# A third bank for the sums of the row maxima, three output banks in place of four, and one more query buffer, in the front of a two-branch attention kernel

## The chip, the cores and the metric

The kernel runs on one core of one Trainium2 chip. The metric is the device time of one execution in microseconds (us). Before the change the median of three runs is 1454.08 us (1453.64 to 1454.22). The profile is of another execution, which took 1453.78 us; its span, from the first to the last instruction, is 1452.0 us. About 0.2%, or 2.9 us, is what a measurement of this kernel can tell from no change.

## The reference

There are 2048 positions and a model width of 512, with 32 heads of 16. Branch A is attention over 8 dilated neighbours of each position; branch B has 32 query heads and one shared key and value head over all 2048 positions. A sigmoid gate mixes the two.

```python
qkv = (x @ wqkv).reshape(B, S, 3, H, Dh).transpose(2, 0, 3, 1, 4)
idx = pos[:, None] - (arange(8) * 2)[None, :]          # branch A: 8 positions, 2 apart
logits = where(idx >= 0, einsum("bhsd,bhswd->bhsw", q, k[idx]) * scale, -1e9)
a = (softmax(logits) @ v[idx]) @ wo

scores = einsum("bhqd,bkd->bhqk", x @ wq, x @ wk) * Dh ** -0.5   # branch B
b = (softmax(scores) @ (x @ wv)) @ wo_b
return g * a + (1 - g) * b                             # g = sigmoid(x . gate_w)
```

## The kernel before

**The units of branch B.** The 2048 queries times 32 heads are 32 units; a unit's queries stand in one buffer `qst[place(u)]`, 128 partitions by 2 x 512. Its upper and its lower 64 partitions hold different queries, so TensorE works on them as two independent row halves: a matmul of one half runs beside a matmul of the other. Before the exponentials of a unit can run, the maximum of its scores over all keys must be known; it is subtracted inside the matmul by two more rows of `qst`. So each unit needs 64 *half scores*: a 128 x 512 block of scores (four blocks of keys, four of queries, two banks of heads, two halves), and the maximum of each row of it. There are 2048 of these.

**Three ways to fill a half score.** A *pair* (`fill_pair`, bank `pm`) is two half scores, one for each row half, and one VectorE reduction of 128 x 1024 (line 365). A *single* (`fill_one`, mostly bank `ps`, that is `m1`) is one matmul on one half and one reduction of 128 x 512 (line 377). A *difference and sum* handles two half scores of the same row half together: a matmul against `kd`, the difference of two blocks of keys (`fill_diff`, line 414, banks `pd`), a Relu of it by ScalarE into a held buffer `dd` (line 426), then a matmul of the second block (`fill_sum`, line 343, banks `ps` or `po`) and one custom VectorE instruction that adds the two and takes the maximum (line 438, followed by a short read of the accumulator). Two matmuls and two half scores in every case; only the difference and sum needs one VectorE instruction for two half scores of one row half.

**The front.** The projections come first: the queries of branch B (13 lumps after the first three) and q, k, v of branch A (64 lumps), each lump 12 products of a split in three terms, each product one matmul for either row half. `front_stream` writes out TensorE's order by hand: it keeps a model clock for each row half and at each point either takes the next projection matmul of that half (`mm`, line 1136) or a fill (`pick`), if by its model a bank is free, the buffers are there and VectorE and ScalarE are not behind. The projections accumulate in four output banks in turn, `fb[x % 4]` (`home`); the upper half of lump x waits until lump x - 4 has left its bank (`below`). Sums of the upper row half use `m1`, those of the lower half `po`. Differences use two banks of their own, `pd`. The numbers at the top of the file (`T_EXP`, `T_TTR` and so on) are the planner's durations; they put no instruction into the program, but they decide its order. Units that have been queued with `stack` can be filled; nine buffers `qst` and one more, `qstx`, stand in memory during the front. In the first 10 us and again between 40 and 60 us GpSimd clears rows 32 to 63 and 96 to 127 of the buffers (`clear`, two memsets of 32 x 1024 each). GpSimd also splits the query projections in two terms (lines 245 and 246); ScalarE can copy the next query projection out only when that is done.

**The steady part.** Then come 512 steps, 16 for each unit. A step on TensorE is four matmuls of scores for exponentials (`exp_pair`, line 486, two into either of two double banks), four matmuls of weighted values (`weighted`, line 501), a pair of half scores, and, in as many steps as are needed to be done in time, a single. ScalarE takes two exponentials of 128 x 1024 in a step (line 492). `singles(s)` decides which steps get a single, from what is still to be filled. In three places four rows of outputs are projected (`out_phase`), with differences and sums in between, and the last four rows end the kernel. Branch A runs on GpSimd beside all this until about 1100 us.

TensorE takes its instructions in order: a fill that waits for its bank holds up both row halves.

Of the kernel before, what the change touches and what calls it, by code (L numbers as in the profile page):

```python
# [35 lines left out]
VN = DH + 2  # L36
NB = 9
NS = NU * NJ
# [5 lines left out]

T_R, T_LAT, T_EXP, T_RED2, T_RED1, T_W, T_TTR = 0.235, 0.20, 0.92, 1.14, 0.61, 1.21, 0.74


@with_exitstack
def gated_mix_kernel(ctx, tc, xt, wa, wk, wq, wo_a, wo_b, out):
    nc = tc.nc  # L50
# [112 lines left out]
    def clear(k, eng):  # L163
        for b in (0, 64):
            eng.memset(qst[k][b + 32:b + 64].bitcast(F32), 0.0)  # L165

    for k in range(4):
        clear(k, nc.gpsimd)
    nc.gpsimd.memset(vst[:, :, 16:32], 1.0)

    idv = ident.rearrange("p (b s d) -> p b s d", b=2, s=4)
# [60 lines left out]
    def queries_post(m, bank, key, ups_at):  # L232

        nonlocal pool
        settle("rest", 0)
        own = p0q.tile([P, 512], F32, name="qraw", bufs=1) if m % 2 else p0.tile([P, 512], F32, name="qraw2", tag="wkr", bufs=1)
        hi, lo = parts_of()
        got = nc.scalar.activation(own, bank, AF.Copy)
        at = after("act", clk["pe"] + T_LAT, 0.62)
        mark(got, at, ups_at)  # L240
        free[key] = at + 0.1

        def rest():
            nonlocal pool
            nc.gpsimd.tensor_copy(hi, own)
            nc.gpsimd.tensor_sub(lo, own, hi.bitcast(F32))
            pool = max(pool, 1e3 * at) + 2300
            queries_out(m, hi, lo)
            if m > 4 and m % 2 and len(stacked) < NB:
                stack(len(stacked))  # L250

        tasks.append((max(pool / 1e3, at), rest, (), "rest"))
# [65 lines left out]
    half = []  # L318
    free = {"m1": 0.0, "e0": 0.0, "e1": 0.0, "po": 0.0, "d0": 24.0, "d1": 24.0}
    tasks, shifted = [], set()  # L320
# [95 lines left out]
    def fill_diff(b, dst, key):  # L416
# [9 lines left out]
        got = nc.scalar.activation(held[b][k], dst, AF.Relu)  # L426
        free[key] = after("act", max(after("pe", 0, T_R) + T_LAT, read_d[b][k]), 0.53) + 0.08
        mark(got, free[key])
# [5 lines left out]
    def fill_sum(b, dst, key):  # L434
        v, pr, t, kc, k, ready = pend[b].pop(0)
        m = unit_tile(v)
        max_mm(dst, v, pr, t, kc + 1, b)
        got = nc.vector.tensor_tensor_reduce(held[b][k], dst, held[b][k], 1.0, -FMAX, ALU.add, ALU.max, m[:, b, pr, t, kc:kc + 1])  # L438
        free[key] = read_d[b][k] = after("dve", max(after("pe", 0, T_R) + T_LAT, ready), T_TTR) + 0.08
        mark(got, free[key])  # L440
        filled(v, 2)
# [552 lines left out]
    for c in range(C):  # L994
        tasks.append((29.0 + 1.5 * c, split_x, (3, nc.gpsimd, [c])))
    for k in range(4, NB):
        tasks.append((37.0 + 3.5 * (k - 4), clear, (k, nc.gpsimd)))

# [106 lines left out]
    def home(x):  # L1105
        if x >= last - 1:
            return ends[x]
        return fb[x % 4], f"f{x % 4}"

# [14 lines left out]
    def begin_exp(k):  # L1124
        free[f"e{k}"] = max(free.get(f"f{y}", 0.0) for y in range(4))
        exp_pair(0, k)
# [69 lines left out]
    def pick(b):  # L1196
        now = clk["pe"]
        if pend[b]:
            key = ("m1", "po")[b]
            if fits(key) and pend[b][0][5] <= now + 0.7 and clk["dve"] <= now + 1.5:  # L1200
                return lambda: fill_sum(b, (m1, po)[b], key)
            if len(pend[b]) == len(held[b]):
                return None
# [59 lines left out]
    def below(x, i):  # L1263
        if i > 0 or x < 4:
            return True
        if x >= last - 1:
            return settled(x)
        return x - 4 in posted and free.get(home(x)[1], 0.0) <= clk["pe"] - 0.05

# [149 lines left out]
```

## Time and profile before

| what | value |
|---|---|
| median of three runs | 1454.08 us |
| the profiled execution, its own time | 1453.78 us |
| its span | 1452.0 us |
| TensorE busy | 1441.8 us (99%) |
| weight loads of TensorE | 733.3 us (51%) |
| ScalarE busy | 1289.8 us (89%) |
| VectorE busy | 1145.4 us (79%) |
| GpSimd busy | 958.8 us (66%) |
| granted TensorE clock | 1.000 |

The front's own matmuls begin 23 us and end 276 us from the start; the steady part ends at about 1430 us. Names are those of the program: `pe`, `pm`, `ps`, `po`, `pd`, `pf` are banks of PSUM (`pf` the output banks of the front), `pexp` the exponentials, `mx` the maxima, `dd` the held differences. In the profile a busy TensorE is one that has a matmul in it, whether its ends meet or not; how much work a stretch holds is seen better by counting matmuls, and which engine sets the pace of a step by the chain of waits.

### The profile page before, as it was taken

How to read it: one execution, taken by the hardware profiler on the slowest of the kernel's cores; microseconds unless marked ns; L12 is line 12 of the kernel's file. 1: busy time of each engine (PE TensorE's matmuls, PEld its weight loads, DVE VectorE, ACT ScalarE, POOL GpSimd, SP SyncE). 2: the span in 40 equal slices, each digit the busy share in tenths (PEclk: the TensorE clock that was granted, in tenths of full speed). 3: DMA queues.
4: the chain of work that ended last, by engine and by line, in shares of the span. 5: the costliest groups of instructions: out<-in, count | busy, mean ns of one | idle time of the engine just before them, and what ended most of it. 6: DMA issues, size and time to landing. Idle time of an engine off the chain costs nothing.

```text
span 1452.0 us, 29592 instructions
## 1 busy us (share of the span) xinstructions
PE 1441.8 (99%) x10985; PEld 733.3 (51%) x10985; DVE 1145.4 (79%) x1851; ACT 1289.8 (89%) x1645; POOL 958.8 (66%) x1718
## 2 busy tenths in 40 slices
PE   9999999999999999999999999999999999999999
PEld 6899999733333333333333373333333743733335
DVE  6888988878888888888888878888888778788821
ACT  6888888789999999999999979999999889799994
POOL 6942998888889888888898897888981211311000
PEclk9999999999999999999999999999999999999999
DMA  7663342411211202012012020211200000000000
GB/s 228 166 175 111 106 149 68 127 49 42 80 38 54 75 16 69 31 39 79 28 64 72 13 93 20 72 43 42 72 12 12 27 16 2 24 9 1 1 2 29
DMA packets 45688, 85.50 MB, mean 59 GB/s; under 512 B 10400, under 2 KB 28376, under 8 KB 41448
## 3 DMA queue, kind: packets, MB, share of 16 engines
q1 hardware_dynamic: 38552, 45.21, 10.3%
q0 software_dynamic: 6560, 37.95, 8.2%
q8 instruction: 86, 1.41, 0.4%
q14 instruction: 58, 0.48, 0.1%
q10 hardware_dynamic: 432, 0.46, 0.1%
HBM read 57.77 MB, written 25.25 MB: 57 GB/s over the span
## 4 chain that ended last, share of the span: by engine, by line
PE 95%; POOL 2%; DVE 1%; issue 1%; ACT 1%; DMA 0%; POOLq 0%; SPq 0%; DVEq 0%; ACTq 0%
PE po L501 34%; PE pe L486 25%; PE pf L1136 10%; PE pm L343 8%; PE ps L343 5%; PE pe L819 5%; PE pd L414 3%; PE po L343 2%; PE pe L1348 1%; POOL qst L165 1%; PE pf L204 0%; POOL tr L570 0%; PE pd L929 0%; POOL pr L564 0%; ACT pexp L492 0%
## 5 line engine op out<-in xcount | busy, mean ns | idle before, releaser
L492 ACT ACTIVATE pexp<-pe 128x1024 f32<-128x1024 f32 x1021 | 984.5, 1023 | 71.0 <-PE pe L486 66.1
L365 DVE TENSOR_REDUCE mx<-pm 128x2 f32<-128x1024 f32 x479 | 584.9, 1221 | 173.0 <-PE pm L343 169.5
L501 PE MATMUL po<-pexp,vst 128*32 128x512 f32 x4096 | 545.5, 605 | 0.1
L486 PE MATMUL pe<-qst,kst 64*128 64x512 f32 x1914 | 496.0, 458 | 3.5 <-DVE other L702 2.7
L486 PEld LDWEIGHTS pe<-qst,kst 64*128 64x128 f32 x1914 | 195.8, 183 | 436.3 <-ACT pexp L492 406.7
L426 ACT ACTIVATE dd<-pd 128x512 f32<-128x512 f32 x376 | 219.4, 602 | 51.9 <-PE pd L414 24.3
L377 DVE TENSOR_REDUCE mx<-ps 128x1 f32<-128x512 f32 x315 | 214.0, 679 | 2.6 <-PE pf L1136 1.2
L343 PE MATMUL ps<-kst,qst 62*128 62x512 f32 x478 | 195.1, 408 | 0.1
L564 POOL TENSOR_TENSOR pr<-aext 128x256 f32<-128x256 f32 x256 | 182.3, 741 | 4.1 <-DMA aext<-ad 3.9
L343 PE MATMUL pm<-kst,qst 62*128 62x512 f32 x883 | 178.1, 397 | 0.1
L624 POOL TENSOR_TENSOR oa<-oa,av 128x256 f32<-128x256 f32 x224 | 164.5, 734 | 15.7
L501 PEld LDWEIGHTS po<-pexp,vst 128*32 128x32 f32 x4096 | 80.6, 108 | 168.5 <-issue 158.9
L621 POOL TENSOR_TENSOR av<-aext,lg 128x256 f32<-128x256 f32 x224 | 139.6, 623 | 12.7
L1136 PE MATMUL pf<-wah,xl 64*128 64x384 f32 (+1 forms) x496 | 147.7, 338 | 0.0
L438 DVE CUSTOM_DVE_ANT_0 dd<-ps,dd 128x512 f32<-128x512 f32 x190 | 131.0, 690 | 20.9 <-PE ps L343 7.4
L438 DVE CUSTOM_DVE_ANT_0 dd<-po,dd 128x512 f32<-128x512 f32 x186 | 128.2, 689 | 23.0 <-PE po L343 10.3
L414 PE MATMUL pd<-kd,qst 62*128 62x512 f32 x368 | 143.4, 398 | 0.4 <-ACT dd L426 0.4
L1136 PE MATMUL pf<-wal,xh 64*128 64x384 f32 (+1 forms) x496 | 141.8, 337 | 0.0
L1136 PE MATMUL pf<-wah,xh 64*128 64x384 f32 (+1 forms) x496 | 137.6, 338 | 0.0
L528 POOL TENSOR_TENSOR rl<-rl,gate_t 128x16 f32<-128x16 f32 x31 | 7.1, 231 | 151.2 <-DVE rl L521 151.0
L343 PEld LDWEIGHTS ps<-kst,qst 62*128 62x128 f32 x478 | 88.4, 185 | 33.9 <-DVE mx L377 27.3
L1136 PEld LDWEIGHTS pf<-wah,xl 64*128 64x128 f32 x496 | 91.1, 186 | 0.2
(219 smaller groups left out, 1795.3 us busy)
## 6 DMA issues: line engine op xcount, KB each, us to landing
aext<-ad POOLq DMA_DIRECT2D x32, 1056.0 KB, 5.5
ad<-stage SPq DMA_DIRECT2D x32, 384.0 KB
qst<-qd SPq DMA_DIRECT2D x60, 128.0 KB
xraw<-xt SPq DMA_DIRECT2D x16, 256.0 KB
qd<-qhi SPq DMA_DIRECT2D x16, 256.0 KB
qd<-qlo SPq DMA_DIRECT2D x16, 256.0 KB
qst<-qd SPq DMA_DIRECT2D x60, 64.0 KB
qst<-ml SPq DMA_DIRECT2D x212, 2.0 KB
```

The source lines that it names most:

```text
L343: nc.tensor.matmul(dst, qst[place(v)][b:b + 62, pr, t * P:(t + 1) * P], kst[b:b + 62, kc * 512:(kc + 1) * 512], start=True, stop=True)
L365: got = nc.vector.tensor_reduce(m[:, :, pr, t, kc], dst, AX.X, ALU.max)
L377: got = nc.vector.tensor_reduce(m[:, odd, pr, t, kc:kc + 1], dst, AX.X, ALU.max)
L414: nc.tensor.matmul(dst, qst[place(v)][b:b + 62, pr, t * P:(t + 1) * P], kd[0][b:b + 62, kc // 2, :], start=True, stop=True)
L426: got = nc.scalar.activation(held[b][k], dst, AF.Relu)
L438: got = nc.vector.tensor_tensor_reduce(held[b][k], dst, held[b][k], 1.0, -FMAX, ALU.add, ALU.max, m[:, b, pr, t, kc:kc + 1])
L486: nc.tensor.matmul(bank[:, odd, :], kst[b:b + 64, kt * P:(kt + 1) * P], qst[place(u)][b:b + 64, pr, :], start=True, stop=True)
L492: got = nc.scalar.activation(e, bank, AF.Exp, scale=SCALE)
L501: nc.tensor.matmul(po[32 * i:32 * i + 32, :], vst[:, kt, :], pexp[s, i // 2][:, i % 2, :], start=(kt == 0), stop=(kt == NJ - 1))
L564: nc.gpsimd.tensor_mul(pr[:, k], q, e[:, o:o + NH, AC:2 * AC])
L624: nc.gpsimd.tensor_add(ao, ao, av)
L1136: inst = nc.tensor.matmul(home(x)[0][:, :n], l[h], r[h], start=(i == 0 and b == 0), stop=(i == 3 * C - 1 and b == 1))
```

## The change

- `home` and `below`: the projections of the front turn through three banks, `fb[0]` to `fb[2]`. The fourth, `fb[3]`, becomes a bank for sums (`"sx"`) that either row half may use when its own bank is not free.
- `NB` goes from 9 to 10: eleven query buffers stand in the front (ten and `qstx`). Room is made by a smaller scratch for the descriptors of GpSimd's DMAs, 8192 in place of 16384 bytes per partition. After query lump 14 a unit is stacked, too.
- `clear` is one memset of the whole buffer, 128 x 1024, in place of two of 32 x 1024. Eight buffers are cleared at the very start, the other two around 50 us.
- The planner's numbers change: `T_TTR` from 0.74 to 0.66, the Relu from 0.53 (and 0.08 until its bank is free) to 0.5 (and 0.17), and the held buffer is counted as free 0.05 later.

```diff
-NB = 9
+NB = 10
-T_R, T_LAT, T_EXP, T_RED2, T_RED1, T_W, T_TTR = 0.235, 0.20, 0.92, 1.14, 0.61, 1.21, 0.74
+T_R, T_LAT, T_EXP, T_RED2, T_RED1, T_W, T_TTR, T_REL = 0.235, 0.20, 0.92, 1.14, 0.61, 1.21, 0.66, 0.5
...
     def clear(k, eng):
-        for b in (0, 64):
-            eng.memset(qst[k][b + 32:b + 64].bitcast(F32), 0.0)
+        eng.memset(qst[k].bitcast(F32), 0.0)
...
     nc.gpsimd.memset(vst[:, :, 16:32], 1.0)
+    for k in range(4, NB - 2):
+        clear(k, nc.gpsimd)
...
-            if m > 4 and m % 2 and len(stacked) < NB:
+            if m > 4 and (m % 2 or m == 14) and len(stacked) < NB:
...
-        free[key] = after("act", max(after("pe", 0, T_R) + T_LAT, read_d[b][k]), 0.53) + 0.08
+        free[key] = after("act", max(after("pe", 0, T_R) + T_LAT, read_d[b][k]), T_REL) + 0.17
...
-        free[key] = read_d[b][k] = after("dve", max(after("pe", 0, T_R) + T_LAT, ready), T_TTR) + 0.08
+        free[key] = after("dve", max(after("pe", 0, T_R) + T_LAT, ready), T_TTR) + 0.08
+        read_d[b][k] = free[key] + 0.05
...
-    for k in range(4, NB):
-        tasks.append((37.0 + 3.5 * (k - 4), clear, (k, nc.gpsimd)))
+    for k in range(NB - 2, NB):
+        tasks.append((50.0 + 4.0 * (k - NB + 2), clear, (k, nc.gpsimd)))
...
-        return fb[x % 4], f"f{x % 4}"
+        return fb[x % 3], f"f{x % 3}"
...
         if pend[b]:
-            key = ("m1", "po")[b]
-            if fits(key) and pend[b][0][5] <= now + 0.7 and clk["dve"] <= now + 1.5:
-                return lambda: fill_sum(b, (m1, po)[b], key)
+            for dst, key in ((m1, "m1"), (po, "po"))[b], (fb[3], "sx"):
+                if fits(key) and pend[b][0][5] <= now + 0.7 and clk["dve"] <= now + 1.5:
+                    return lambda: fill_sum(b, dst, key)
...
-        return x - 4 in posted and free.get(home(x)[1], 0.0) <= clk["pe"] - 0.05
+        return x - 3 in posted and free.get(home(x)[1], 0.0) <= clk["pe"] - 0.05
...
-    nc = bacc.Bacc("TRN2", target_bir_lowering=False, num_devices=1)
+    nc = bacc.Bacc("TRN2", target_bir_lowering=False, num_devices=1, dynamic_dma_scratch_size=8192)
```

What the planner makes of it shows in TensorE's order. The first place is in the front, in the middle of branch A's projections. `pf_97` to `pf_100` are the four output banks before, `pd_92` and `pd_93` the two banks for differences. Before:

```order
L1136 MATMUL pf_99<-wal,xh 128x384
L343 MATMUL po<-kst,qst_81 128x512
L414 MATMUL pd_92<-kd,qst_81 128x512
L1136 MATMUL pf_97<-wah,xh_120 128x384
L1136 MATMUL pf_99<-wah,xl 128x384
L1136 MATMUL pf_97<-wal,xh_120 128x384
L1136 MATMUL pf_99<-wah,xh 128x384
L414 MATMUL pd_93<-kd,qst_82 128x512
L1136 MATMUL pf_99<-wal,xh 128x384
L343 MATMUL ps<-kst,qst_81 128x512
```

In the changed program the numbers of these banks are one higher: `pf_98` to `pf_100` are the output banks, `pf_101` is the bank "sx", and two more lines of code stand ahead of line 1138. A piece of the front there:

```order
L1138 MATMUL pf_98<-wal,xh 128x402
L344 MATMUL pf_101<-kst,qst_79 128x512
L1138 MATMUL pf_100<-wah,xh 128x402
L1138 MATMUL pf_98<-wah,xl 128x402
L1138 MATMUL pf_100<-wal,xh 128x402
L1138 MATMUL pf_98<-wah,xh 128x402
L344 MATMUL ps<-kst,qst_79 128x512
L1138 MATMUL pf_98<-wal,xh 128x402
L1138 MATMUL pf_100<-wah,xl 128x402
L415 MATMUL pd_94<-kd,qst_79 128x512
```

A sum now goes to a third bank, and another sum follows six matmuls later. Over the whole front, from the first projection matmul of line 1136 to the last, TensorE's order holds 2517 matmuls where it held 2458: 30 more sums and other scores (340 for 310) and 29 more differences (321 for 292); the 1848 projections stay. VectorE has 321 custom sums there for 292.

The second place is the steady part, steps 214 to 216 of 512. Before, two steps with a single (`ps`) in a row, and one without:

```order
L501 MATMUL po<-pexp,vst 32x512 x4
L486 MATMUL pe_4193<-qst_78,kst 128x512 x2
L343 MATMUL pm<-kst,qst_76 128x512 x2
L343 MATMUL ps<-kst,qst_76 128x512
L486 MATMUL pe_4194<-qst_78,kst 128x512 x2
L501 MATMUL po<-pexp,vst 32x512 x4
L486 MATMUL pe_4193<-qst_78,kst 128x512 x2
L343 MATMUL pm<-kst,qst_76 128x512 x2
L343 MATMUL ps<-kst,qst_76 128x512
L486 MATMUL pe_4194<-qst_78,kst 128x512 x2
```

The changed program at the same steps:

```order
L503 MATMUL po<-pexp,vst 32x512 x4
L488 MATMUL pe_4339<-qst_77,kst 128x512 x2
L344 MATMUL pm<-kst,qst_82 128x512 x2
L344 MATMUL ps<-kst,qst_82 128x512
L488 MATMUL pe_4340<-qst_77,kst 128x512 x2
L503 MATMUL po<-pexp,vst 32x512 x4
L488 MATMUL pe_4339<-qst_77,kst 128x512 x2
L344 MATMUL pm<-kst,qst_82 128x512 x2
L488 MATMUL pe_4340<-qst_77,kst 128x512 x2
```

The second step has lost its single. Over the steady part the single steps go from 304 to 237, and steps without a single (*bare* steps) from 177 to 244. A bare step directly behind a bare one comes 26 times for 12, a single step behind a single one 22 times for 140. The three output phases hold 86 differences for 80 and 95 sums and singles for 93, eight matmuls more. In all the program has as many matmuls as before.

On GpSimd eight buffers are cleared ahead of its first other work (before: four, by eight memsets), and two memsets stand where ten stood between 40 and 60 us.

More of the change, by code (lines that the diff above doesn't have):

```diff
@@ L318, in gated_mix_kernel @@
     half = []
-    free = {"m1": 0.0, "e0": 0.0, "e1": 0.0, "po": 0.0, "d0": 24.0, "d1": 24.0}
+    free = {"m1": 0.0, "e0": 0.0, "e1": 0.0, "po": 0.0, "d0": 24.0, "d1": 24.0, "sx": 24.0}
     tasks, shifted = [], set()
@@ L1124, in begin_exp @@
     def begin_exp(k):
-        free[f"e{k}"] = max(free.get(f"f{y}", 0.0) for y in range(4))
+        free[f"e{k}"] = max(free.get(y, 0.0) for y in ("f0", "f1", "f2", "sx"))
         exp_pair(0, k)
@@ L1263, in below @@
     def below(x, i):
-        if i > 0 or x < 4:
+        if i > 0 or x < 3:
             return True
```

## The prediction

> **What bounds the kernel now.** I read the page first, for the engines' shares and the chain that ended last.
>
> ```profile
> PE 1441.8 (99%) x10985; PEld 733.3 (51%) x10985; DVE 1145.4 (79%) x1851; ACT 1289.8 (89%) x1645; POOL 958.8 (66%) x1718
> ...
> PE 95%; POOL 2%; DVE 1%; issue 1%; ACT 1%; DMA 0%; POOLq 0%; SPq 0%; DVEq 0%; ACTq 0%
> ```
>
> TensorE is on the chain for 95% of the span, yet the change takes no matmul out of the program. So the question is what one matmul costs in the front and what it costs in the steady part. The busy times of one stretch of each (columns: length, PE, weight loads, VectorE, ScalarE, GpSimd, clock, DMA share, GB/s) say this:
>
> ```profile
> 100.00:250.00 150.00, 149.99 (x1560) 146.56 (x1558) 133.48 (x396) 128.01 (x259) 103.40 (x205) 1.00 0.36 110
> ...
> 690.00:790.00 100.00, 100.00 (x712) 36.39 (x708) 83.31 (x99) 94.75 (x105) 86.29 (x160) 1.00 0.15 48
> ```
>
> A busy PE may still have room, so I take the chain of waits of six steps, by the starts of the weighted values (`po`); the rows between are the step's other matmuls, and a step is single if `ps` stands in it:
>
> ```profile
> 337.19 1.00 PE po L501 x8
> 338.19 0.43 PE pe L486 x2
> 338.62 0.23 PE pm L343 x2
> 338.85 0.23 PE ps L343
> 339.09 0.24 PE pe L486 x2
> 339.32 0.99 PE po L501 x8
> ...
> 341.22 0.99 PE po L501 x8
> ...
> 342.87 0.41 PE pe L486 x2
> 343.28 0.55 PE po L501
> ...
> 617.30 0.99 PE po L501 x8
> ...
> 619.19 1.00 PE po L501 x8
> ...
> 620.90 0.23 PE ps L343
> ...
> 621.39 1.00 PE po L501 x8
> ...
> 623.05 0.26 PE ps L343
> ...
> 623.55 0.55 PE po L501
> ```
>
> The first step has a single: 339.32 - 337.19 = 2.13 us, matmul after matmul, with no wait in it. The next is bare: 1.90. The third is bare behind a bare one: 2.06, and the excess sits in its last scores (0.41 for 0.24), which wait for a bank that ScalarE still reads. In the second piece come a bare step of 1.89 and two single ones of 2.20 and 2.16. So the steady part is bound by TensorE, a single costs its time in full, and ScalarE is close behind:
>
> ```profile
> 336.77 3.83 ACT L492 ACTIVATE pexp<-pe 128x1024 f32<-128x1024 f32 x4 [0.25 <-PE pe L486]
> 340.79 2.92 ACT L492 ACTIVATE pexp<-pe 128x1024 f32<-128x1024 f32 x3 [0.19 <-PE pe L486]
> ```
>
> One more exponential adds 3.83 - 2.92 = 0.91 us, so two need 1.82, below a bare step's 1.90. ScalarE holds only where bare steps follow each other and its other work falls in.
>
> In the front a matmul runs beside one of the other row half. The groups of the same 150 us:
>
> ```profile
> L414 PE MATMUL pd<-kd,qst 62*128 62x512 f32 x188 | 74.1, 394 | 0.0
> L343 PE MATMUL po<-kst,qst 62*128 62x512 f32 x94 | 37.2, 396 | 0.0
> L343 PE MATMUL ps<-kst,qst 62*128 62x512 f32 x94 | 37.0, 394 | 0.0
> ```
>
> That is 376 fills of 512 columns; the other 1184 of 1560 are projections of 384 columns (some of 402). At the 0.235 us that a 512-column matmul takes in the chain above (0.23 to 0.24), and 384/512 of it for a projection, both halves need (376 x 0.235 + 1184 x 0.176) / 2 = 148 of the 150 us. The front is full as well: there is no hole into which a fill could go for nothing.
>
> **The change part by part.** The orders give the counts: 59 more fills in the front, 67 singles fewer in the steps, 8 fills more in the output phases.
>
> *Steps.* 67 steps lose their single. The three single steps above take 2.16 in the mean, the two bare ones behind a single 1.895, a difference of 0.27; the cleanest pair gives 0.23. I take 0.26, near the mean since single steps in a row, the slower kind, almost vanish (22 for 140): 67 x 0.26 = -17.4 us, bounds 67 x 0.23 = -15.4 and 67 x 0.27 = -18.1. Against it, 14 more bare steps come behind a bare one, at 2.06 - 1.90 = 0.16 each: +2.2, bounds 0 (ScalarE has caught up) and twice that. ScalarE's cover for the rest: a single and a bare step in turn leave it 4.03 us for four exponentials, 3.64 us. Together -15.2.
>
> *Front.* 59 fills on two row halves, each half 29.5 x 0.235 = +6.9 us. The bounds are 0, if the halves still have holes, and the case that VectorE cannot keep up (first rival). I take 6.9, by the count of 148 in 150. That the projections have three banks for four I cost at nothing: 77 lumps in 253 us are 3.3 us each, a copy out is one ScalarE instruction (0.60 for `qraw<-pf` in a row below), so three banks still let the upper half run most of two lumps ahead; if that cover is gone, TensorE waits up to 0.60 at each lump, 46 us at the very most.
>
> *Memsets.* GpSimd's rows of the first microseconds:
>
> ```profile
> 1.37 7.93 POOL L165 MEMSET qst<- 32x1024 f32 x8
> 9.37 0.32 POOL L169 MEMSET vst<- 128x256 f32 x1
> 15.07 2.99 POOL L82 TENSOR_TENSOR xl<-xraw,xh 128x512 fp32r<-128x512 f32 x2 [5.39 <-DMA dd<-wq]
> ```
>
> A memset of 32 x 1024 takes 0.99 here. One of 128 x 1024 isn't in the trace; by columns it is about 1 us, and four times the 128 x 256 row bounds it at 1.28. Eight of them and `vst` end at 1.37 + 8 x 1.28 + 0.32 = 11.9 at the latest, still under the idle time until 15.07: cost nothing. Later, two memsets stand where ten stood, which takes about 7 us off GpSimd's queue between 40 and 60 us. There it was late once, with ScalarE and TensorE behind it:
>
> ```profile
> 62.92 0.60 ACT L238 ACTIVATE qraw<-pf 128x512 f32<-128x512 f32 x1 [0.98 <-POOL qlo L246]
> ```
>
> ```profile
> 63.28 0.40 PE L1136 MATMUL pf<-xh,wql 64*128 64x512 f32 x1
> 64.06 0.50 PE L414 MATMUL pd<-kd,qst 62*128 62x512 f32 x1 [0.38 <-ACT dd L426]
> ```
>
> From 63.28 to 64.06 is 0.78 where 0.235 was due. I take -0.5 for this stall, bounds 0 and -0.8; next behind it is the chain of difference, Relu and sum itself.
>
> *Output phases.* 8 fills more, on halves that run together: 4 x 0.235 = +0.9, at most 1.9 if nothing runs beside them.
>
> *Scratch.* GpSimd's DMAs bring branch A's data, and DMA has 0% of the chain above: there is nothing to gain, and a later load has to come late by more than GpSimd's idle time (13.7 of 100 us in the stretch above) before TensorE sees it. Nothing. The eleventh buffer costs nothing either: stacking it takes four DMAs on SP that were issued later before.
>
> Sum: -15.2 + 6.9 - 0.5 + 0.9 = -7.9 us. The profiled execution's 1453.78 becomes 1445.9; the median lies 0.3 above it, so 1446.2.
>
> **Rivals.** *VectorE, not TensorE, sets the pace of the front (slower).* It has these groups there, in 100 to 250 us and in the whole front:
>
> ```profile
> L438 DVE CUSTOM_DVE_ANT_0 dd<-ps,dd 128x512 f32<-128x512 f32 x94 | 64.9, 691 | 6.5 <-PE ps L343 0.5 <-ACT dd L426 0.3
> ...
> L438 DVE DVE_READ_ACCUMULATOR2_ANT mx<- 128x1 f32 x188 | 15.5, 83 | 0.0
> ```
>
> ```profile
> L438 DVE CUSTOM_DVE_ANT_0 dd<-po,dd 128x512 f32<-128x512 f32 x147 | 101.3, 689 | 15.6 <-PE po L343 5.4 <-ACT dd L426 1.8 <-PE ps L343 0.7
> L438 DVE CUSTOM_DVE_ANT_0 dd<-ps,dd 128x512 f32<-128x512 f32 x145 | 100.1, 690 | 10.9 <-PE ps L343 1.9 <-ACT dd L426 0.5 <-PE pd L414 0.4
> ```
>
> The front of 253 us has 292 sums, one per 0.866 us; with 321 in 260 it is one per 0.81, in the stretch of 150 us 188 x 321/292 = 207 in 154, 0.75 for 0.80. VectorE is busy 133.48 us for 188 sums, 0.71 each, so at 0.75 it would be nearly full. If it, or the way of a sum through its bank, cannot go below today's pace, the front grows with its sums, 253 x 321/292 = 278, +25 for +6.9: -15.2 + 25 - 0.5 + 0.9 = +10.2, 1464.3. The gain is gone from a front that grows by 15. Against it: neighbours on VectorE overlap.
>
> ```profile
> 844.03 0.69 DVE L678 TENSOR_TENSOR qst<-pe,qst 128x512 fp32r<-128x512 f32 x1
> 844.63 0.68 DVE L377 TENSOR_REDUCE mx<-po 128x1 f32<-128x512 f32 x1
> 845.23 0.68 DVE L438 CUSTOM_DVE_ANT_0 dd<-ps,dd 128x512 f32<-128x512 f32 x1
> ```
>
> Each starts 0.60 behind the one before, though each lasts 0.68 to 0.69. So VectorE can go lower than 0.71 when it has a queue, and a third bank gives it one. Chance 5%.
>
> *No overlap at all (about the same).* VectorE's first sum, and two smaller groups of 100 to 250 us:
>
> ```profile
> 32.48 0.69 DVE L438 CUSTOM_DVE_ANT_0 dd<-po,dd 128x512 f32<-128x512 f32 x1
> ```
>
> ```profile
> L353 DVE TENSOR_REDUCE ms<-mx 128x32 f32<-128x128 f32 x6 | 1.7, 286 | 0.2
> L585 DVE TENSOR_REDUCE amx<-lg 128x16 f32<-128x128 f32 x4 | 1.5, 372 | 0.0
> ```
>
> If a sum (0.69) and its read (0.083) had to end before the next starts, 321 x 0.773 = 248 us from 32.5 on reach 280.6; the two groups add 5.5 in the whole front, and I put as much again for what is smaller and for singles: the front ends at 291.6, 15.5 later than now. -15.2 + 15.5 - 0.5 + 0.9 = +0.7, 1454.8. Against it stand the 0.60 above, and 188 x 0.773 = 145 us of durations in 133.48 busy. Chance 5%. This is what the Trainium skill's page "VectorE: DVE Perf Modes", section "The DRAIN you can't avoid", would give: the next operation does not start until the pipeline has emptied. The trace does not agree for these three operations; the page itself sends the reader on to operations that are not held.
>
> *The steady part is not bound by TensorE (slower).* Its weight loads are busy 36 of 100 us there, 147 of 150 in the front; if the steps were paced by ScalarE (94.75 of 100), taking singles away would bring nothing and the front would cost its full price: 6.9 - 0.5 + 0.9 = +7.3, 1461.4. Against it stand bare steps of 1.90 beside single ones of 2.13. Chance 3%. The Trainium skill's page "Perfetto Trace Analysis", section "Identifying the Most-Contended Engine", calls the matmuls' busy share a bad measure of TensorE's headroom and would have it judged by the weight loads' share; by that rule the change moves work from where TensorE has room to where it has none. The chain of waits speaks against using it so here.
>
> *The front takes the fills for nothing.* Then -14.8, 1439.3; against it 148 of 150 us. Chance 5%.
>
> **How the numbers follow.** The forecast has 82%. Its own bounds, -18.1 + 5 - 0.8 + 0.9 = -13 and -15.4 + 4.4 + 9 + 1.9 = 0 (the front between 5 and 9 us), are ends that hardly come together; I give 1442.5 to 1451.5, which leaves out the four rivals (18%) and the corners of the forecast (some 2%). A measurement tells 0.2% (2.9 us) from no change. Faster: the forecast but for 1%, and the free front, 86%. Same: 6%, the no-overlap case and that 1%. Slower: 8%, the first and the third rival.
>
> **What would show it.** Right: the last projection of the front some 6 to 7 us later than 276; single steps 2.13 to 2.16 and bare ones 1.90, 237 and 244 of them; no idle TensorE near 64 us; sums in the front's middle at 0.75 us. Wrong: differences or sums of the front waiting for VectorE with TensorE idle, a front beyond 290 us, or bare steps at 2.0 and more throughout.

## The result

| | time, us (range, runs) | profiled execution, its span |
|---|---|---|
| before | 1453.78 (1453.62 to 1454.22, 6) | 1453.78, 1452.0 |
| after | 1441.72 (1441.32 to 1442.54, 6) | 1441.69, 1439.9 |

The ratio is 0.9917, 95% interval [0.9904, 0.993]: 12.1 us faster. The prediction said 7.9 us faster, 1446.2, with a range down to 1442.5. The direction held, and so did both sides of the sum, a longer front and shorter steps; the time lies 0.8 us below the range.

**The profile after.** The page's shares of the engines, and its chain:

```profile
PE 1430.7 (99%) x10985; PEld 748.2 (52%) x10985; DVE 1120.1 (78%) x1851; ACT 1299.8 (90%) x1679; POOL 946.9 (66%) x1708
...
PE 97%; ACT 1%; issue 1%; DMA 0%; DVE 0%; SPq 0%; ACTq 0%; DVEq 0%
```

As many matmuls as before are 11 us shorter in busy time, and GpSimd, 2% of the chain before, is gone from it. Busy times by stretch (columns: length, PE, weight loads, VectorE, ScalarE, GpSimd, clock, DMA share, GB/s):

```profile
100.00:250.00 150.00, 149.40 (x1542) 147.31 (x1540) 134.45 (x421) 129.84 (x271) 104.22 (x207) 1.00 0.35 106
690.00:790.00 100.00, 99.89 (x716) 37.18 (x713) 79.42 (x93) 95.51 (x106) 85.33 (x153) 1.00 0.15 48
```

The front is as full as it was, so 59 more fills make it longer: its last projection ends at 282.4 us (276.1 before). The steady part is what became shorter. Its chain of waits, where three single steps were looked at before:

```profile
337.08 0.99 PE po L503 x8
...
338.97 0.99 PE po L503 x8
...
340.63 0.22 PE ps L344
...
341.08 1.00 PE po L503 x8
...
342.98 0.99 PE po L503 x8
...
344.63 0.23 PE ps L344
...
345.11 1.00 PE po L503 x8
...
701.27 0.99 PE po L503 x8
...
702.93 0.47 PE pe L488 x2
703.40 0.99 PE po L503 x8
```

Bare and single steps now take turns, at 1.89, 2.11, 1.90 and 2.13 us: no single here costs the 2.16 and 2.20 of the two dear ones read before. The last piece is a bare step behind a bare one, with 2.13 the price of a single; 0.23 of that is in its last scores (0.47 for 0.24).

All steps of both traces, measured from the start of their weighted values to the next start, and what lies between these stages:

| | before | after | difference |
|---|---|---|---|
| front: first start to last end of the projections | 23.2 to 276.1 | 22.8 to 282.4 | +6.3 at the end |
| from there to the first weighted values | 0.7 | 1.2 | +0.5 |
| single steps | 304, mean 2.161: 656.9 | 237, mean 2.139: 507.0 | -149.9 |
| bare steps | 177, mean 1.922: 340.2 | 244, mean 1.927: 470.2 | +130.0 |
| steps of the output phases and others | 155.5 | 156.5 | +1.0 |
| span | 1452.0 | 1439.9 | -12.1 |

Single and bare steps together: -19.9 us, where the prediction had -15.2. That is the whole miss and a little more.

GpSimd's first microseconds:

```profile
1.26 3.62 POOL L164 MEMSET qst<- 128x1024 f32 x4
4.83 0.30 POOL L168 MEMSET vst<- 128x256 f32 x1
5.08 3.62 POOL L164 MEMSET qst<- 128x1024 f32 x4
14.67 2.99 POOL L82 TENSOR_TENSOR xl<-xraw,xh 128x512 fp32r<-128x512 f32 x2 [5.97 <-ACT xh L81]
```

Eight whole buffers end at 8.7 us, six before the next work. VectorE's groups in the front's middle, 100 to 250 us:

```profile
L439 DVE CUSTOM_DVE_ANT_0 dd<-ps,dd 128x512 f32<-128x512 f32 x72 | 49.6, 689 | 7.0 <-PE ps L344 2.4 <-ACT dd L427 1.5 <-PE po L344 1.0
L439 DVE CUSTOM_DVE_ANT_0 dd<-po,dd 128x512 f32<-128x512 f32 x64 | 44.0, 688 | 6.0 <-PE po L344 2.4 <-PE ps L344 0.8 <-PE pf L1138 0.5
L439 DVE CUSTOM_DVE_ANT_0 dd<-pf,dd 128x512 f32<-128x512 f32 x64 | 43.9, 686 | 0.7 <-PE pf L344 0.2
```

The third row is the new bank: a third of the 200 sums. They come every 0.75 us (150 / 200), and VectorE still idles and waits for TensorE; the other way round there is one stall of TensorE in these 150 us, of 0.60 us at 173.5.

### The profile page after: what moved, and what is told of

Its sections match the earlier page's. It is cut to its first block, busy times and chain, and to the rows that moved or that the text cites. A ratio compares the mean times of both kernels' runs of the same rounds, so it can differ in the third digit from the quotient of the medians.

```text
span 1439.9 us, 29642 instructions
## 1 busy us (share of the span) xinstructions
PE 1430.7 (99%) x10985; PEld 748.2 (52%) x10985; DVE 1120.1 (78%) x1851; ACT 1299.8 (90%) x1679; POOL 946.9 (66%) x1708
## 3 DMA queue, kind: packets, MB, share of 16 engines
q1 hardware_dynamic: 38552, 45.21, 10.2%
## 4 chain that ended last, share of the span: by engine, by line
PE 97%; ACT 1%; issue 1%; DMA 0%; DVE 0%; SPq 0%; ACTq 0%; DVEq 0%
PE po L503 35%; PE pe L488 24%; PE pf L1138 11%; PE pm L344 8%; PE ps L344 5%; PE pe L821 4%; PE pd L415 4%; PE po L344 1%; ACT pexp L494 1%; PE pf L344 1%; PE pe L1350 1%; PE pd L931 0%; DMA xraw<-xt 0%; PE pm L879 0%; PE pf L205 0%
## 5 line engine op out<-in xcount | busy, mean ns | idle before, releaser
L488 PE MATMUL pe<-qst,kst 64*128 64x512 f32 x1914 | 477.1, 460 | 3.8 <-DVE other L704 3.2
L488 PEld LDWEIGHTS pe<-qst,kst 64*128 64x128 f32 x1914 | 185.5, 183 | 452.6 <-ACT pexp L494 413.4
L427 ACT ACTIVATE dd<-pd 128x512 f32<-128x512 f32 x410 | 231.7, 603 | 49.9 <-PE pd L415 39.6
L626 POOL TENSOR_TENSOR oa<-oa,av 128x256 f32<-128x256 f32 x224 | 164.1, 733 | 15.5
L378 DVE TENSOR_REDUCE mx<-ps 128x1 f32<-128x512 f32 x246 | 167.2, 680 | 2.6 <-PE pe L821 1.4
L415 PE MATMUL pd<-kd,qst 62*128 62x512 f32 x405 | 156.9, 395 | 0.0
L344 PE MATMUL ps<-kst,qst 62*128 62x512 f32 x387 | 154.6, 400 | 0.6 <-DVE mx L439 0.6
L439 DVE CUSTOM_DVE_ANT_0 dd<-ps,dd 128x512 f32<-128x512 f32 x164 | 113.0, 689 | 29.1 <-PE ps L344 12.4
L439 DVE CUSTOM_DVE_ANT_0 dd<-po,dd 128x512 f32<-128x512 f32 x146 | 100.5, 688 | 11.3 <-PE po L344 4.5
L1138 PEld LDWEIGHTS pf<-wah,xh 64*128 64x128 f32 x496 | 87.4, 186 | 0.4
L1138 PEld LDWEIGHTS pf<-wal,xh 64*128 64x128 f32 x496 | 87.0, 186 | 0.1
```

Source lines behind the costliest of these rows:

```text
L344: nc.tensor.matmul(dst, qst[place(v)][b:b + 62, pr, t * P:(t + 1) * P], kst[b:b + 62, kc * 512:(kc + 1) * 512], start=True, stop=True)
L378: got = nc.vector.tensor_reduce(m[:, odd, pr, t, kc:kc + 1], dst, AX.X, ALU.max)
L415: nc.tensor.matmul(dst, qst[place(v)][b:b + 62, pr, t * P:(t + 1) * P], kd[0][b:b + 62, kc // 2, :], start=True, stop=True)
L488: nc.tensor.matmul(bank[:, odd, :], kst[b:b + 64, kt * P:(kt + 1) * P], qst[place(u)][b:b + 64, pr, :], start=True, stop=True)
L626: nc.gpsimd.tensor_add(ao, ao, av)
L1138: inst = nc.tensor.matmul(home(x)[0][:, :n], l[h], r[h], start=(i == 0 and b == 0), stop=(i == 3 * C - 1 and b == 1))
```

## The experiments

**Theories.** *Neighbours*: a single is worth 0.23 us by itself, but a single behind a single loses about 0.05 more and a bare step behind a bare one about 0.15, so the order of the steps counts beside their number. *Flat*: each single is worth the same 0.26 or so, wherever it stands, and the rest of the gain is in the front (its stalls). Of the parts of the change it is asked which of them makes the gain.

Measured times are medians; the difference is against before on the same chip. "Fills" are those that the order moves to the front; "0-0" are bare steps behind bare ones, "1-1" singles behind singles (without the first 21 steps); "idle" is the idle time of the upper and the lower row half in the front, from the starts of each half's matmuls.

| kernel | us | ratio, 95% | difference | fills | front ends | idle | singles | 0-0 | 1-1 |
|---|---|---|---|---|---|---|---|---|---|
| before | 1453.78 | | | 0 | 276.1 | 7.6, 8.2 | 304 | 10 | 133 |
| after | 1441.72 | 0.9917 [0.9904, 0.993] | -12.1 | 59 | 282.4 | 6.8, 8.3 | 237 | 24 | 21 |
| after_again | 1441.42 | 0.9914 [0.9901, 0.9928] | -12.3 | 59 | 282.1 | | 237 | 24 | 21 |
| memset_only | 1451.42 | 0.9986 [0.9977, 0.9995] | -2.1 | 0 | 275.2 | 6.8, 7.0 | 304 | 10 | 133 |
| numbers_only | 1447.96 | 0.9962 [0.9947, 0.9976] | -5.6 | 25 | 281.4 | 11.6, 11.0 | 259 | 21 | 57 |
| bank_only | 1452.33 | 0.9992 [0.9982, 1.0001] | -1.2 | 35 | 282.3 | 9.5, 11.8 | 268 | 23 | 76 |
| no_buffer | 1446.64 | 0.9953 [0.9939, 0.9967] | -6.9 | 38 | 281.6 | 6.8, 9.5 | 256 | 24 | 56 |
| no_third_bank | 1446.79 | 0.9958 [0.9945, 0.9972] | -7.0 | 25 | 280.2 | 10.4, 9.8 | 259 | 21 | 57 |
| old_memsets | 1445.98 | 0.9949 [0.9932, 0.9965] | -7.7 | 59 | 285.5 | 10.2, 11.4 | 237 | 24 | 21 |
| old_numbers | 1448.41 | 0.9964 [0.995, 0.9978] | -5.4 | 35 | 282.4 | 9.4, 10.1 | 268 | 16 | 69 |
| clustered | 1455.35 | 1.0013 [1.0004, 1.0023] | +1.6 | 59 | | | 233 | 115 | 106 |
| left_out | 1438.13 | 0.9898 [0.9881, 0.9914] | -15.6 | 0 | 275.5 | | 230 | 48 | 31 |
| x_m05 | 1449.82 | 0.9975 [0.9965, 0.9984] | -3.9 | 99 | 289.2 | 11.2, 10.0 | 193 | 99 | 8 |
| odd_steps | 1436.75 | 0.9884 [0.987, 0.9897] | -17.0 | 59 | 283.0 | 7.0, 7.9 | 241 | 0 | 2 |

### The steps

**clustered**: the same front; only which steps get a single is changed, so that they come two by two.

```diff
-        owing[0] = min(owing[0], 3.0)
+        owing[0] = min(owing[0], 4.0)
...
-        if s % 16 == 0 or owing[0] < 1.0 or clk["dve"] - clk["pe"] > 1.5 and owing[0] < 2.0:
+        if s % 16 == 0:
             return False
+        if s - 1 in paired_at:
+            return True
+        if owing[0] < 2.0 or s % 16 == 15:
+            return False
+        paired_at.add(s)
         return True
```

> The changed kernel with the singles of the steps put in twos: 233 singles (for 237), single behind single 110 times (for 22), bare behind bare 121 (for 26); the front is untouched. Theory 'neighbours': -1 + 88 x 0.05 + 95 x 0.15 = +17.7 us against the changed kernel, so +5.7 against before. Flat price for a single and nothing for its neighbours: -1 against the changed kernel, -13 against before.

It is 13.6 us slower than after, though it has 4 singles fewer: the flat theory (-1) is out, and the other's 17.7 is 4.1 too much. The chain of waits of five steps, from their weighted values:

```profile
702.66 0.99 PE po L503 x8
...
704.32 0.53 PE pe L488 x2
704.85 0.99 PE po L503 x8
...
706.51 0.24 PE pe L488 x2
706.75 0.99 PE po L503 x8
...
708.41 0.39 PE pe L488 x2
708.81 1.00 PE po L503 x8
```

These bare steps take 2.19 (the first, behind a single), 1.90 and 2.06 us; whatever is lost is lost in the last scores (0.53 and 0.39 for 0.24), which go into a bank that ScalarE has to empty. ScalarE's row at the same time:

```profile
704.13 1.94 ACT L494 ACTIVATE pexp<-pe 128x1024 f32<-128x1024 f32 x2 [0.19 <-PE pe L488]
706.31 5.93 ACT L494 ACTIVATE pexp<-pe 128x1024 f32<-128x1024 f32 x6 [0.25 <-PE pe L488]
```

Six exponentials without a gap take 5.93, more than three bare steps of 1.90 (5.70). So in a row of bare steps ScalarE sets the pace. Over the trace 115 bare steps behind bare ones lose 14.8 us against 1.896, 0.13 each; 106 singles behind singles lose 5.0 against 2.128, 0.05 each. In the means of the steps' matmuls, the loss of a single behind a single is at the single's own matmul (0.28 for 0.235 to the next start). The waits of its weight load from 500 to 800 us (in total, times, longest), of before, after and clustered, show what it waits for:

```profile
PEld ps L343 <- DVE mx L377: 8.0, 36, 0.3
```

```profile
PEld ps L344 <- DVE mx L378: 1.1, 5, 0.3
```

```profile
PEld ps L344 <- DVE mx L378: 6.7, 31, 0.2
```

It is VectorE's reduction of the single before it, which still reads the bank `ps`. In these 300 us there are 37, 6 and 35 singles behind singles; odd_steps has none there, and no such wait.

**left_out**: before, with 67 half scores of the steady part left out.

```diff
...
+    def leave_out():
+        if not half:
+            v, pr, t, kc = slots.pop(0)
+            half.extend([(v, pr, t, kc, 0), (v, pr, t, kc, 1)])
+        v = half.pop(0)[0]
+        unit_tile(v)
+        filled(v, 1)
+        dropped[0] += 1
...
```

> The kernel before with 67 half scores of the steady part left out (their matmul and their maximum are not made, so some maxima lack a block of keys); the front is untouched. 74 singles fewer in the steps, 6 fills more in the output phases, single behind single 32 times for 140, bare behind bare 50 for 12. If a single costs its time in the steady part: -17.8 - 5.4 + 5.7 + 0.7 = -16.8 us against before. If the steps are not paced by TensorE (the third rival): no change.

This is nearly the steps' part of the change, with nothing in the front to pay for it: -15.6 us for the -16.8 expected, with 74 singles fewer but 48 bare steps behind bare ones, which lose 6.7 us. No change, as it would be if TensorE did not pace the steps, is out.

**x_m05**: after, with a front that takes still more.

```diff
-LEAD, M2S, M1S, MARGIN = 1.75, 0.5, 0.3, 0.12
+LEAD, M2S, M1S, MARGIN = 1.75, 0.5, 0.3, 0.05
```

> The changed kernel with the planner's margin of 0.05 for 0.12: 40 fills more in the front, 14 more in the output phases and 44 singles fewer in the steps (193 for 237), but bare behind bare 103 times for 26. Theory 'neighbours': -10.6 + 11.5 + 4.7 + 1.6 - 0.5 = +6.7 us against the changed kernel. Flat price with no cost for bare neighbours: -10.6 + 6.3 = -4.3 us, a faster kernel. A smaller margin may also make fills wait for their banks in the front.

40 more fills, 44 singles fewer, and 8.1 us slower than after, where neighbours had 6.7 and the flat price a gain of 4.3. The front ends 6.8 us later (40 / 2 x 0.235 = 4.7 for the matmuls, the rest is idle time), and 99 bare steps behind bare ones lose 13.2 us, 9.6 more than in after. So a fuller front is no gain by itself; past after's counts each single that goes makes more than one bare step stand behind a bare one (75 more for 44 singles).

**odd_steps** and **after_again**: the change improved. The rule that picks the steps is cut to odd steps, with the even ones as a reserve; after_again is the changed kernel on the same chip.

```diff
-        if s % 16 == 1:
-            return True
-        if s % 16 == 0 or owing[0] < 1.0 or clk["dve"] - clk["pe"] > 1.5 and owing[0] < 2.0:
-            return False
-        return True
+        if s % 2:
+            return owing[0] > -2.0
+        return s % 16 > 0 and owing[0] >= 2.9
```

> After, with the singles of the steady part put on odd steps only, so that almost none stands next to another: 241 singles for 237, 240 bare steps for 244, no bare step behind a bare one (26 before), 2 singles behind singles (22 before); the front has the same 59 fills. Neighbours (a bare step behind a bare one loses about 0.15 us, a single behind a single 0.05): -26 x 0.15 - 20 x 0.05 + 4 x 0.23 = -4.0, 1437.7 us if after gives 1441.7. Flat (every single the same, wherever it stands): +4 x 0.23 = +0.9, 1442.6 us. The output phases get 2 bundles fewer of 89, which is worth less than 0.5 by either.

> After once more, for a comparison on the same chip: 1441.7 us by every theory, within 0.3.

1436.75 against 1441.42: -4.7 us with 4 singles more, where the flat theory had +0.9. Its chain of waits, single and bare in turn:

```profile
691.31 1.00 PE po L503 x8
...
693.44 0.99 PE po L503 x8
...
695.33 1.00 PE po L503 x8
...
697.45 1.00 PE po L503 x8
...
699.35 1.00 PE po L503 x8
```

The steps are 2.13, 1.89, 2.12 and 1.90. No bare step follows a bare one (3.6 us of losses gone); singles behind singles 1.0 to 0.1, the first 21 steps 1.1 to 0.5; four singles more cost 0.9. Of all kernels that compute the whole reference this is the fastest.

### The parts

The diffs below are against before for the parts alone, against after for the parts taken out.

**memset_only**:

```diff
-        for b in (0, 64):
-            eng.memset(qst[k][b + 32:b + 64].bitcast(F32), 0.0)
+        eng.memset(qst[k].bitcast(F32), 0.0)
...
-    for k in range(4, NB):
-        tasks.append((37.0 + 3.5 * (k - 4), clear, (k, nc.gpsimd)))
+    for k in range(NB - 2, NB):
+        tasks.append((50.0 + 4.0 * (k - NB + 2), clear, (k, nc.gpsimd)))
```

> The kernel before with only the memsets changed (one of 128 x 1024 per buffer, those of buffers 4 to 6 moved to the start); TensorE's order is unchanged. Theory 'neighbours' (the 4 us beyond the forecast come from single steps that no longer follow each other): only the stall near 64 us goes and GpSimd's start gets shorter, -0.5 to -1 us against before. Rival 'stalls' (the 4 us come from GpSimd being earlier, which also clears the stalls of the first steps, at 296 and 307 us): -3 to -4 us, and steps 9 and 14 at 2.1 us or less, where they took 3.53 and 2.83.

-2.1, between the two: the front ends 0.9 earlier, and the first 21 steps lose 2.1 us instead of 3.2, though their order is the same. The rival had expected this second part, only larger: of its two steps the one of 3.53 falls to 2.33 and not to 2.1, and the one of 2.83 stays. What holds the first of them shows on VectorE and TensorE of before, and on VectorE of memset_only:

```profile
296.72 0.25 DVE L598 RECIPROCAL asum<-asum 128x16 f32<-128x16 f32 x1 [1.92 <-POOL asum L608]
296.89 1.16 DVE L365 TENSOR_REDUCE mx<-pm 128x2 f32<-128x1024 f32 x1
```

```profile
298.11 0.50 PE L343 MATMUL pm<-kst,qstx 62*128 62x512 f32 x2 [0.79 <-DVE mx L365]
```

```profile
294.61 0.25 DVE L599 RECIPROCAL asum<-asum 128x16 f32<-128x16 f32 x1 [0.73 <-POOL asum L609]
```

A reciprocal of branch A waits for GpSimd, 1.92 us in before and 0.73 here; the maxima behind it in VectorE's queue wait with it, and TensorE (0.79) for their bank. In after VectorE has no wait for GpSimd from 283 to 330 us.

**numbers_only** and **bank_only**:

```diff
-T_R, T_LAT, T_EXP, T_RED2, T_RED1, T_W, T_TTR = 0.235, 0.20, 0.92, 1.14, 0.61, 1.21, 0.74
+T_R, T_LAT, T_EXP, T_RED2, T_RED1, T_W, T_TTR, T_REL = 0.235, 0.20, 0.92, 1.14, 0.61, 1.21, 0.66, 0.5
...
+        read_d[b][k] = free[key] + 0.05
```

```diff
-        return fb[x % 4], f"f{x % 4}"
+        return fb[x % 3], f"f{x % 3}"
...
+            for dst, key in ((m1, "m1"), (po, "po"))[b], (fb[3], "sx"):
```

> The kernel before with only the planner's numbers changed (T_TTR 0.66, Relu 0.5 and 0.17, held buffer 0.05 later). The order now has 25 fills more in the front, 18 more in the output phases, 45 singles fewer in the steps, single behind single 62 times for 140, bare behind bare 23 for 12. Theory 'neighbours' (0.24 us for a single, 0.05 for a single behind a single, 0.15 for a bare behind a bare, 0.12 for a fill that runs beside another): -10.8 - 3.9 + 1.7 + 2.9 + 2.1 = -8.0 us. By the prediction's flat prices (0.26 for a single, 0.16 for a bare behind a bare): -4.9. If the numbers are too short for the hardware, sums wait for their bank in the front and the gain is smaller than either.

> The kernel before with only the third bank for sums (three output banks), old numbers and ten buffers. The order has 35 fills more in the front, 8 more in the output phases, 36 singles fewer, single behind single 82 times for 140, bare behind bare 24 for 12. Theory 'neighbours': -8.6 - 2.9 + 1.8 + 4.1 + 0.9 = -4.7 us. Flat prices: -9.4 + 1.9 + 4.1 + 0.9 = -2.5. If three output banks hold the projections up, the front grows by more than 4 us.

-5.6 and -1.2. Bank_only's front grows by 6.2, over the 4 named; this run does not tell whether the three output banks or something else holds it up. Both fronts end nearly as late as after's, for 25 and 35 fills where after has 59: each half idles some 3 us more. With banks alone there is almost nothing left of the gain; the interval touches 1. The expectations of the neighbours theory (-8.0 and -4.7) had counted the fills and not this idle time; the others (-4.9 and -2.5) come closer, but by luck: in numbers_only the single and bare steps gave -12.8 (1.1 of it in the first 21), where neighbours had -13.0 and the flat prices -9.9, so that a gain too small made up for a front too short.

**no_buffer**: after without the eleventh buffer (`NB = 9`, no stack at query lump 14, the old scratch).

```diff
-NB = 10
+NB = 9
...
-            if m > 4 and (m % 2 or m == 14) and len(stacked) < NB:
+            if m > 4 and m % 2 and len(stacked) < NB:
...
```

> The changed kernel without the eleventh query buffer (NB 9, scratch as before). The order stops at 316 differences in the front (for 321), where the ten buffers are used up; 48 singles fewer than before (for 67), single behind single 62, bare behind bare 24. Theory 'neighbours': -11.5 - 3.9 + 1.8 + 4.5 + 2.0 - 1 = -8.1 us against before, so 4 us slower than the changed kernel. If the buffer only brought room that nobody needs, it is as fast as the changed kernel, -12.

-6.9: without the buffer the front runs out of queries and takes 38 fills for 59. The buffer and the smaller scratch together bring 5.2 us; what the scratch alone costs was not measured.

**no_third_bank**: after with four output banks again.

```diff
-        return fb[x % 3], f"f{x % 3}"
+        return fb[x % 4], f"f{x % 4}"
...
-            for dst, key in ((m1, "m1"), (po, "po"))[b], (fb[3], "sx"):
+            key = ("m1", "po")[b]
...
```

> After with four output banks and no third bank for sums, as before had them; the numbers, the memsets and the eleventh buffer as in after, and with them the same counts: 59 fills moved to the front, 237 singles, 244 bare steps, 26 bare behind bare. If the idle time of the kernel with the numbers alone (11.6 and 11.0 us in the two row halves, for 6.8 and 8.3 in after) came from GpSimd being late with the old memsets and the projection steps behind them, this front ends within 1 us of after's 282.4 and the time is 1441.7 to 1442.5. If the third bank is what lets 59 sums go in without idle time, the front ends 3 to 5 us later than after's and the time is 1445 to 1447.

1446.79, the second of the two times, but the expectation was wrong about the kernel: the trace has 259 singles and 222 bare steps, the planner moves only 25 fills without the bank. So it doesn't tell what 59 fills would do with two banks for sums; it tells that without the third bank the planner, which never starts a sum before its model has a bank free, doesn't place them, and that this is worth 5.1 us.

**old_memsets**: after with before's memsets.

```diff
-        eng.memset(qst[k].bitcast(F32), 0.0)
+        for b in (0, 64):
+            eng.memset(qst[k][b + 32:b + 64].bitcast(F32), 0.0)
...
-    for k in range(NB - 2, NB):
-        tasks.append((50.0 + 4.0 * (k - NB + 2), clear, (k, nc.gpsimd)))
+    for k in range(4, NB):
+        tasks.append((37.0 + 3.5 * (k - 4), clear, (k, nc.gpsimd)))
```

> After with the query buffers cleared as in before (two memsets of 32 rows each, four buffers at the start, the others from 37 us on, one every 3.5 us); the numbers, the banks and the eleventh buffer as in after, and with them the same 59 fills, 237 singles and 244 bare steps. If the parts add, the memsets are worth here what they were worth with the numbers and four output banks (1447.96 - 1446.79 = 1.2 us) or alone (2.1 us): 1442.9 to 1443.8 us. If only their own stall of 0.5 us counts, 1442.2 us. If a fuller front feels a late GpSimd more than a spare one, 1444.5 us or more.

-7.7, so the memsets are worth 4.4 us here and 2.1 alone; the third expectation holds. Of the 3.9 by which its span is longer (1443.8) the front has 3.1, by its end; single and bare steps, as many as in after, have 1.0. Busy times from 50 to 72 us, of old_memsets and of after:

```profile
50.00:72.00 22.00, 19.44 (x163) 17.16 (x161) 16.59 (x53) 15.84 (x31) 20.80 (x27) 1.00 0.60 170
```

```profile
50.00:72.00 22.00, 22.00 (x192) 21.81 (x190) 19.34 (x61) 18.84 (x37) 17.35 (x24) 1.00 0.59 160
```

GpSimd 20.80 for 17.35 of 22 us, and TensorE loses 2.6. How it comes about, on GpSimd, ScalarE and TensorE of old_memsets:

```profile
57.50 1.94 POOL L165 MEMSET qst<- 32x1024 f32 x2
59.40 0.56 POOL L131 DMA_DIRECT2D waraw<-wa  x1
60.00 0.15 POOL L337 MEMSET mx<- 128x64 f32 x1
60.09 0.61 POOL L245 CAST qhi<-qraw 128x512 fp32r<-128x512 f32 x1
60.79 1.29 POOL L246 TENSOR_TENSOR qlo<-qraw,qhi 128x512 fp32r<-128x512 f32 x1
```

```profile
62.11 0.60 ACT L238 ACTIVATE qraw<-pf 128x512 f32<-128x512 f32 x1 [1.85 <-POOL qlo L246]
62.60 2.28 ACT L426 ACTIVATE dd<-pd 128x512 f32<-128x512 f32 x4
```

```profile
63.25 0.50 PE L414 MATMUL pd<-kd,qst 62*128 62x512 f32 x1 [1.28 <-ACT dd L426]
```

The memsets stand ahead of the split of a query lump; ScalarE's copy of the next lump waits 1.85 us for the split, and the Relus behind it in ScalarE's queue wait with it; TensorE waits 1.28 for the first of them. The same comes again at 69 us. Before has it once and shorter (0.38 at 64 us).

**old_numbers**: after with the old numbers of the planner.

```diff
-T_R, T_LAT, T_EXP, T_RED2, T_RED1, T_W, T_TTR, T_REL = 0.235, 0.20, 0.92, 1.14, 0.61, 1.21, 0.66, 0.5
+T_R, T_LAT, T_EXP, T_RED2, T_RED1, T_W, T_TTR = 0.235, 0.20, 0.92, 1.14, 0.61, 1.21, 0.74
...
```

> After with the old numbers of the front's bookkeeping (0.74 for a sum, 0.53 and 0.08 for the copy, no 0.05), everything else as in after. The order moves 35 fills to the front instead of 59 and leaves 268 singles and 213 bare steps, of which 17 stand behind a bare one; 73 singles stand behind singles. If the memsets and the banks take the idle time away (as in after) and the fills pay their steps: 35 / 2 x 0.235 = +4.1 in the front, -36 x 0.23 - 60 x 0.05 + 7 x 0.15 = -10.2 in the steps, so -6 to -7 against before, 1447 us. If the front idles as that of the kernel with the banks alone (9.5 and 11.8 us): +2.8 on that, 1449.5 to 1450 us.

1448.41, between the two, with idle times between as well. The numbers are worth 6.7 us in the changed kernel.

So the parts do not add. Alone they bring 5.6, 2.1 and 1.2 us, 8.9 together (the buffer alone wasn't run). Taken out of the whole, each of these costs more than it brings alone: 6.7 (numbers), 4.4 (memsets), 5.1 (bank); the buffer taken out costs 5.2. A fill needs a bank, a buffer, a planner that believes in it and a GpSimd that is not late; whichever of these is short, the others bring less.

## Why the prediction was too small

The step that failed is *Steps*: -15.2 forecast, -19.9 measured. It had the right mechanism and two terms of the wrong size: the singles that stay, which it took to cost what they cost before, and the first 21 steps, which it put at nothing without a reason. The losses over 2.128 us of a single and 1.896 of a bare step (the medians in before, of a single behind a bare step and of a bare step behind a single), summed over all steps, say where the difference is:

| what | forecast | measured |
|---|---|---|
| 67 singles removed | -17.4 (67 x 0.26) | -15.5 (67 x 0.232) |
| singles that no longer stand behind singles | in the 0.26 | -5.1 (6.1 for 133, now 1.0 for 21) |
| bare behind bare | +2.2 | +2.1 (1.5 for 10, now 3.6 for 24) |
| bare behind single | 0 | +1.5 (1.5 for 159, now 3.0 for 206) |
| single behind bare | 0 | -0.6 |
| the first 21 steps | 0 | -2.2 (3.25, now 1.07) |

I saw that singles in a row were the slower kind (of the two dear steps that I read, only the one of 2.16 is one; that of 2.20 stands behind a bare step), put that into the price of one single (0.26 for 0.23), and multiplied it by the 67 that go. But 112 fewer stand behind another. If all 67 that go were of these, 45 more stay singles and become 0.046 cheaper each, 2.1 us; and those that go were then worth 0.232 + 0.046 = 0.28 for 0.26, another 1.2 us. Together that is the 5.1 of the second row but for the 1.9 that the dearer price had allowed for. The upper bound, 67 x 0.27, had the same fault. clustered and odd_steps show the two prices at work, in either direction, with the number of singles almost held (233 and 241 for 237).

The first 21 steps were not looked at. In before one of them takes 3.53 us (at 295.8) and one 2.83 (at 307.4). Their loss is 0.4 to 3.2 us over the kernels here and changes when the front or GpSimd shifts, as in memset_only, where their order is the same. The step of 3.53 is VectorE's wait for GpSimd shown there; what holds that of 2.83 stays open.

These 2.2 us are nearly half of the 4.7 by which *Steps* was too small. Without them the time would be some 1443.9 us (1441.7 + 2.2), inside the range: the wrong price alone would not have carried it out. The prediction's own lower bound, -13 (1441.1 us), would have held the time too, but with a front of 5 us where 6.3 was measured.

The other steps, in the prediction's order:
- *Front*, +6.9: +6.3 at its end, +6.7 in its length. The count of 148 in 150 us was the right bound.
- *Three output banks*, 0: right for the whole change, the idle time of the halves is 6.8 and 8.3 us for 7.6 and 8.2. There is a new stall of 0.60 at 173.5, for a bank of sums and not of outputs; that of 64 us is gone.
- *Memsets*, 0 at the start and -0.5: the start is right. The 0.5 is what the stall cost in before; for the changed kernel the edit decided over two stalls of 1.28 us that before does not have. That does not alter the sum, which was made with all parts in, but whoever had judged the parts by their own prices would have left this one out.
- *Output phases*, +0.9: +0.4 (99.8 to 100.2), +1.0 with the other steps. From the front to the first weighted values +0.5, which the sum did not have.
- *Eleventh buffer*, no cost: not measured apart from its worth, which was not asked for; the buffer and the smaller scratch together bring 5.2 us.

The rivals. VectorE as the bound of the front: out, 200 sums in 150 us with VectorE idle between them. No overlap on VectorE: out for these operations, as VectorE's own row in after shows.

```profile
120.60 0.69 DVE L439 CUSTOM_DVE_ANT_0 dd<-po,dd 128x512 f32<-128x512 f32 x1
121.22 0.08 DVE L439 DVE_READ_ACCUMULATOR2_ANT mx<- 128x1 f32 x1
121.24 0.69 DVE L439 CUSTOM_DVE_ANT_0 dd<-ps,dd 128x512 f32<-128x512 f32 x1
```

The next sum starts 0.64 behind this one, though a sum and its read last 0.77 together. The Trainium skill's page "VectorE: DVE Perf Modes", section "The DRAIN you can't avoid", lets the next operation start only when the pipeline is empty, but says too that one that is not held starts earlier; here it starts earlier, by these rows.

A steady part that TensorE does not bound: out as well, by left_out. But ScalarE is so close that it bounds the bare steps in a row. Weight loads are busy 37 of 100 us in the steady part and 147 of 150 in the front, and the work that moved to the front was still gained. The Trainium skill's page "Perfetto Trace Analysis", section "Identifying the Most-Contended Engine", would have TensorE's headroom judged by MFU, its share of the peak arithmetic, and by the busy share of the weight loads. The latter would have misled here; MFU was not worked out.

A front that takes fills for nothing: out, by 6.3 us.

## What to carry to other kernels

When instructions are removed from a repeated step, price the steps by their neighbours, and count for each kind of pair how many there are before and after: the change of those that stay belongs into the sum. Where other engines are nearly level with the bounding one (here ScalarE in light steps, VectorE in heavy ones), let heavy and light steps take turns; that was worth 4.7 us here, with four singles more. Look at the first repetitions apart from the rest. Price an enabling edit (a buffer, a bank, an earlier memset) inside the whole change, by taking it out, and not alone.

## What was not expected of the hardware

- A memset of 128 x 1024 on GpSimd takes 0.91 us (3.62 for four), one of 32 x 1024 takes 0.99 (7.93 for eight): four times the rows cost nothing, so two memsets of 32 rows cost twice one of the whole buffer.
- Six exponentials of 128 x 1024 in a row took 5.93 us, 0.99 each; in the prediction I had taken 0.91 for one more, from two shorter rows, so that ScalarE seemed to have room in a bare step.
- A kernel whose order of steps is the same word for word can lose 1 us more or less in the first 21 steps when its front ends 0.9 us earlier, because work of another branch waits on VectorE ahead of the steps' own (1.92 us, then 0.73).
